# A zeroed 128x512 tile on GpSimd between the record scatters of an attention and mixture-of-experts kernel

## The chip, the cores and the metric

The kernel runs on one core of a Trainium2 chip. The metric is device microseconds (us) of one execution, the median of several runs; less is better.

## What is computed

```python
def _attn_ref(q, k, v):                       # 8 batches, 8 heads, 576 tokens, head size 64
    k_p = k.reshape(B, H, Sp, pool, D).mean(axis=3)      # pool = 8, Sp = 72
    v_p = v.reshape(B, H, Sp, pool, D).mean(axis=3)
    scores = scale * np.matmul(q, k_p.transpose(0, 1, 3, 2))
    attn = np.exp(scores - np.max(scores, axis=-1, keepdims=True))
    attn = attn / (np.sum(attn, axis=-1, keepdims=True) + 1e-09)
    return np.matmul(attn, v_p)

def _moe_ref(x, w_gate, w_noise, noise, w1, w2):  # x: 4608 tokens of 512; 8 experts of 512x1024 and 1024x512
    noisy_logits = x @ w_gate + np.log1p(np.exp(x @ w_noise)) * noise
    top2 = np.argpartition(-noisy_logits, 2, axis=1)[:, :2]
    ...
    for e in range(E):
        for k in range(2):
            mask = top2[:, k] == e
            h = np.maximum(x[mask] @ w1[e], 0.0)
            out[mask] += top2_w[mask, k, None] * (h @ w2[e])
```

The attention's output, laid out by tokens, is x of the second function. All of it is float32.

## The kernel before, in words

The program has two stages. In the first the eight batches are taken in four pairs (`pr` 0 to 3). A pair is nine chunks of 128 tokens, so there are 36 chunks. In a chunk TensorE transposes q (`qp`, L347), multiplies it by the pooled keys (`s`, L375), VectorE takes the maximum of each row (`mx`, L380), ScalarE the exponential (`ex`, L382), TensorE transposes the exponentials (`ep`, L393), ScalarE copies them out of PSUM (`eT`, L395), TensorE multiplies them by the pooled values (`a`, L408), and VectorE divides and writes the tokens (`rd` L414, `xr` L419) and their logits (`lg` L421). The string of letters in L116 sets the order in which the steps of neighbouring chunks are issued. PSUM holds two banks of each kind, so TensorE can be about a chunk ahead of the engines that empty them.

When the nine chunks of a pair are done, `route` (L494) works out for each token its two experts, its weights and its place in an expert's list. It is a generator: a few of its VectorE instructions are issued behind each following chunk, so the routing of a pair runs under the chunks of the next. For the first two pairs its opening additions (L509, L510) run on GpSimd, and VectorE's L517 waits for them. At its end it puts 18 scatters (9 columns, 2 experts for each token) into the list `scq`. A scatter (L638) is an indirect DMA that GpSimd issues: 128 records of 16 bytes go from `rec` to the rows of `rec_dram` that `pos` names. The function `advance` (L782) takes one or two from the list at fixed points of each chunk, and each scatter waits for one instruction of ScalarE or VectorE of that point:

```python
            tc.add_manual_dep(s.ins, pace[0].ins.name,
                              mybir.DependencyInfo(mybir.DependencyClass.Sync, mybir.DependencyReason.DATA),
                              reason="paced")
```

Behind the scatters of pair 1 the list holds the load of the first records (`load_recs`, L679) and the gather of the first tokens (`fetch`, `gather`, L706): GpSimd loads `raw`, then issues four indirect DMAs into `xg`. TensorE transposes these in L756, during the last two chunks of the stage. Pair 2 has the same for two more tiles. The 18 scatters of pair 3 are issued in the second stage.

In the second stage (`stage1` L1004, `stage2` L1080) each expert's tokens are multiplied by its two weight matrices. L968 sets three tiles `pv` of 128x512 to zero on GpSimd when the stage begins.

Each engine runs its own instructions in the order in which they stand in the program. GpSimd's queue in the first stage holds, apart from the scatters, the opening additions of two pairs and the gathers.

Of the kernel before, what the change touches and what calls it, by code (L numbers as in the profile page):

```python
# [8 lines left out]
F32 = mybir.dt.float32  # L9
# [10 lines left out]
def kernel(  # L20
# [12 lines left out]
    nc = tc.nc  # L33
    B, H, S, D = q.shape
    NTOK, DM = out.shape
    E = moe_w_gate.shape[1]
    DF = moe_w1.shape[2]
    P = 128
# [38 lines left out]
    rec_dram = dp.tile([E * ER, RW], I32, name="rec_dram")  # L77
# [32 lines left out]
    ap_ = ctx2.enter_context(tc.tile_pool(name="att", bufs=1))  # L110
# [379 lines left out]

    scq = []
    pace = [None]

    def route(pr, c0, c1, lg, psum):  # L494
        n = c1 - c0
# [72 lines left out]
        rec = rp.tile([P, NCH, 2, RW], I32, tag="rec", name=f"rec{pr}_{c0}", bufs=4)  # L568
# [47 lines left out]
        pos = rp.tile([P, 2, NCH], I32, tag="pos", name=f"pos{pr}_{c0}", bufs=4)  # L616
# [18 lines left out]
        V.tensor_add(word(2), later, tb)  # L635

        def scatter(c, i):
            s = nc.gpsimd.indirect_dma_start(  # L638
                out=rec_dram[:, :],
                out_offset=bass.IndirectOffsetOnAxis(ap=pos[:, i, c:c + 1], axis=0),  # L640
                in_=rec[:, c, i, :], in_offset=None)
            tc.declare_no_dep(s.ins, group="rec_scatter", reason="distinct rows")
            if pr >= NP // 2:
                tc.declare_no_dep(s.ins, group="rec_load0", reason="rows of the other half")
            if pr == NP - 1:
                tc.declare_no_dep(s.ins, group="rec_load1", reason="rows of the other pairs")
            tc.add_to_no_dep_group("rec_scatter", s.ins)
# [4 lines that stand above are left out]
        for c in range(n):  # L652
            for i in range(2):
                scq.append(lambda c=c, i=i: scatter(c, i))
# [127 lines left out]
    def advance(n, m):  # L782
        for _ in range(n):
            while gens:
                try:
                    next(gens[0])
                    break
                except StopIteration:
                    gens.pop(0)
        for _ in range(min(m, len(scq))):  # L790
            scq.pop(0)()
# [38 lines left out]
    for b in range(1, B):  # L830
        c = 9 * (b // 2) + (0 if b % 2 == 0 else 4)
# [11 lines left out]
    for b in range(2, B):  # L843
        c = 9 * ((b - 2) // 2) + (0 if b % 2 == 0 else 4)
# [87 lines left out]
            gens.append(route(pr, 0, 5, lgs[pr], one))  # L932
    due.pop()()
    advance(100, 0)
    ctx2.close()


# [308 lines left out]
    with tc.For_i(0, totr, 1) as it:  # L1246
# [5 lines left out]
        rec = op.tile([P, RW], I32, name="orec")  # L1252
# [7 lines left out]
            out=xg, out_offset=None, in_=x_dram[:, :],  # L1260
            in_offset=bass.IndirectOffsetOnAxis(ap=rec[:, 0:1], axis=0))
# [3 lines left out]
            out=pv, out_offset=None, in_=slot_dram[:, :],  # L1265
            in_offset=bass.IndirectOffsetOnAxis(ap=rec[:, 3:4], axis=0))
# [13 lines left out]
        for f in range(NFB):  # L1280
# [5 lines left out]
            out=out, out_offset=bass.IndirectOffsetOnAxis(ap=rec[:, 2:3], axis=0),  # L1286
            in_=res, in_offset=None, bounds_check=NTOK - 1, oob_is_err=False)
# [28 lines left out]
```

## Time and profile before

| what | value |
|---|---|
| median of 3 runs | 1044.02 us (1043.8 to 1044.55) |
| span of the profiled execution, first to last instruction | 1041.8 us |
| time of the profiled execution as a run | not listed apart; the median of the runs is 2.2 us above its span |
| TensorE (PE) busy | 995.3 us, 96% |
| weight loads (PEld) | 889.2 us, 85% |
| VectorE (DVE) busy | 549.0 us, 53% |
| ScalarE (ACT) busy | 345.5 us, 33% |
| GpSimd (POOL) busy | 371.0 us, 36% |
| record scatters (L638) | 72, 76.2 us, mean 1058 ns |

Busy times are sums over the whole span. The first stage ends at about 212 us, where the first matmul of L1017 stands. In a row of the timeline the first number is the start in us from the span's beginning, the second the time from the start of the first to the end of the last instruction of the row; the square bracket holds how long the engine was idle before it, and what ended that. "issue" means that the profile shows no wait that ended there, "remote" that it shows a signal but not who sent it. A matmul's end is modelled, not recorded. PEclk is the granted share of TensorE's full clock.

### The profile page before, as it was taken

The numbers are of one execution on the slowest core, as the hardware profiler recorded it, in microseconds if no ns is written. First come the engines' busy times: TensorE is split into PE (matmuls) and PEld (weight loads), VectorE is DVE, ScalarE is ACT, GpSimd is POOL, SyncE is SP. The second block draws the span as 40 slices with busy tenths as digits, with TensorE's granted clock in tenths as the row PEclk, the third lists the DMA queues.
The fourth block names the chain that finished last, engine by engine and source line by source line (L and its number), as shares of the span: only waits on it lengthen the run. The fifth ranks groups of instructions, "written<-read, shape, count | busy, mean of one in ns | idle before, by whom it ended". The sixth has DMA issues, their size and how long they took to land.

```text
span 1041.8 us, 16452 instructions
## 1 busy us (share of the span) xinstructions
PE 995.3 (96%) x5832; PEld 889.2 (85%) x5832; DVE 549.0 (53%) x1277; ACT 345.5 (33%) x857; POOL 371.0 (36%) x419
## 2 busy tenths in 40 slices
PE   7998989699999999999999999999999999999996
PEld 5897878587998898888988898889888988898995
DVE  5798768494343554554445445444554455456242
ACT  5786667541123122321232123212321232124120
POOL 4024462537310433154215421542154215421514
PEclk9999989799999999999999999999999999999999
DMA  9997853244615656577348736773577357844624
GB/s 277 336 305 235 274 155 103 82 138 118 181 60 144 211 191 191 144 242 219 111 131 249 233 120 170 249 227 100 151 248 245 116 142 258 249 137 142 203 88 136
DMA packets 137382, 190.36 MB, mean 183 GB/s; under 512 B 29155, under 2 KB 84084, under 8 KB 137274
## 3 DMA queue, kind: packets, MB, share of 16 engines
q1 hardware_dynamic: 111834, 121.84, 38.8%
q0 software_dynamic: 25440, 67.05, 20.6%
q8 instruction: 72, 1.18, 0.5%
q14 instruction: 36, 0.29, 0.1%
HBM read 126.07 MB, written 70.74 MB: 189 GB/s over the span
## 4 chain that ended last, share of the span: by engine, by line
PE 88%; issue 3%; ACT 2%; DVE 1%; DMA 1%; POOL 1%; another core or an unknown queue 1%; SPq 1%; POOLq 0%; DVEq 0%; ACTq 0%
PE bank L1017 37%; PE bank L1128 27%; PE bank L1094 10%; PE a L408 5%; PE s L375 3%; PE ep L393 2%; PE qp L347 2%; ACT ex L382 1%; DMA v<-in_v_dram 1%; ACT eT L395 1%; POOL out_dram L1073 1%; PE kT L298 0%; PE vr L325 0%; SPq L219 0%
## 5 line engine op out<-in xcount | busy, mean ns | idle before, releaser
L1017 PE MATMUL bank<-xh,w 128*128 128x512 f32 (+6 forms) x1536 | 390.4, 338 | 0.6 <-issue 0.6
L1017 PEld LDWEIGHTS bank<-xh,w 128*128 128x128 f32 x1536 | 270.3, 188 | 21.4 <-issue 0.9
L1128 PE MATMUL bank<-w,hh 128*128 128x512 f32 x880 | 271.7, 390 | 1.3 <-issue 1.2
L1017 PE MATMUL bank<-xl,w 128*128 128x512 f32 (+6 forms) x768 | 259.7, 338 | 1.2 <-issue 0.9
L1028 ACT ACTIVATE hh<-bank 128x512 fp32r<-128x512 f32 (+4 forms) x192 | 96.7, 510 | 459.9 <-PE bank L1017 369.2
L1029 DVE SCALAR_TENSOR_TENSOR hl<-bank,hh 128x512 fp32r<-128x512 f32 (+4 forms) x192 | 110.1, 579 | 243.1 <-ACT hh L1028 212.7
L1128 PEld LDWEIGHTS bank<-w,hh 128*128 128x128 f32 x880 | 164.8, 188 | 34.8 <-issue 1.1
L1128 PE MATMUL bank<-w,hl 128*128 128x512 f32 x440 | 171.4, 390 | 1.0 <-issue 1.0
L1017 PEld LDWEIGHTS bank<-xl,w 128*128 128x128 f32 x768 | 144.6, 188 | 11.3 <-DVE xl L767 0.6
L1065 DVE SCALAR_TENSOR_TENSOR pv<-bank,raw,pv 128x128 f32<-128x128 f32 x196 | 55.5, 342 | 111.8 <-DMA pv<-slot_dram,raw 51.8
L1069 POOL DMA_DIRECT2D slot_dram<-yt x17 | 9.8, 576 | 276.0 <-DVE yt L1065 225.5
L638 POOL DMA_INDIRECT rec_dram<-rec,pos x72 | 76.2, 1058 | 85.3 <-DVE rec L635 26.9
L1094 PE MATMUL bank<-hh,w 128*128 128x240 f32 (+3 forms) x512 | 103.6, 298 | 2.2 <-issue 1.7
L1128 PEld LDWEIGHTS bank<-w,hl 128*128 128x128 f32 x440 | 82.6, 188 | 19.5 <-issue 2.4
L1049 POOL DMA_INDIRECT pv<-slot_dram,raw x70 | 68.7, 982 | 62.4 <-DMA slot_dram<-ys 34.2
L481 DVE TENSOR_TENSOR w<-wst,w 128x512 fp32r<-128x512 f32 x128 | 82.6, 682 | 11.1 <-ACT w L480 10.6
L1094 PEld LDWEIGHTS bank<-hh,w 128*128 128x128 f32 x512 | 82.6, 189 | 2.7 <-issue 2.1
L480 ACT CAST w<-wst 128x512 fp32r<-128x512 f32 x128 | 73.0, 618 | 27.1 <-DMA wst<-in_moe_w_dram 27.1
L715 POOL DMA_INDIRECT row<-x_dram,raw x70 | 70.2, 1004 | 21.3 <-issue 20.7
L1069 POOL DMA_DIRECT2D slot_dram<-pv x55 | 31.7, 576 | 125.1 <-DVE pv L1065 89.2
L1094 PE MATMUL bank<-hl,w 128*128 128x320 f32 (+3 forms) x256 | 76.0, 297 | 0.0
L382 ACT ACTIVATE ex<-s,mx 128x72 f32<-128x72 f32 x288 | 70.8, 342 | 12.8 <-DVE mx L380 7.5
(165 smaller groups left out, 1032.3 us busy)
## 6 DMA issues: line engine op xcount, KB each, us to landing
wst<-in_moe_w_dram SPq DMA_DIRECT2D x64, 512.0 KB
via<-row SPq DMA_DIRECT2D x266, 64.0 KB
xg<-via SPq DMA_DIRECT2D x63, 256.0 KB
slot_dram<-pv POOLq DMA_DIRECT2D x55, 256.0 KB
k<-in_k_dram SPq DMA_DIRECT2D x7, 1280.0 KB
v<-in_v_dram SPq DMA_DIRECT2D x16, 512.0 KB
x_dram<-xr SPq DMA_DIRECT2D x16, 512.0 KB
q<-in_q_dram SPq DMA_DIRECT2D x7, 1024.0 KB
```

The costliest lines, as they stand in the source:

```text
L382: lasta[0] = nc.scalar.activation(ex[:, jj, EPOS[h] * G:(EPOS[h] + 1) * G], sv[:, i], AF.Exp, bias=mx[:, i:i + 1])
L480: nc.scalar.copy(hv, sv)
L481: nc.vector.tensor_sub(lv, sv, hv.bitcast(F32))
L638: s = nc.gpsimd.indirect_dma_start(out=rec_dram[:, :], out_offset=bass.IndirectOffsetOnAxis(ap=pos[:, i, c:c + 1], axis=0), in_=rec[:, c, ...
L715: turn_of("pool", lambda: nc.gpsimd.indirect_dma_start(out=row[:32 * nr], out_offset=None, in_=x_dram[:, :], in_offset=bass.IndirectOffset ...
L1017: nc.tensor.matmul(part(ph), w1s(e, a, db, f), part(xs[b][:, db]), start=(i == 0), stop=(i == 3 * NDB - 1))
L1028: act = nc.scalar.activation(hh[:, :n], ph[:, :n], AF.Relu)
L1029: last = nc.vector.scalar_tensor_tensor(hl[:, :n], ph[:, :n], 0.0, hh[:, :n].bitcast(F32), op0=OP.max, op1=OP.subtract)
L1049: turn_of("pool", lambda: nc.gpsimd.indirect_dma_start(out=pv[:np_], out_offset=None, in_=slot_dram[:P + e * CAP, :], in_offset=bass.Indir ...
L1065: nc.vector.scalar_tensor_tensor(r_, y_, wc, pv[:plain] if plain else r_, op0=OP.mult, op1=OP.add)
L1094: nc.tensor.matmul(part(py), w2s(e, b, f)[:, mb * P:(mb + 1) * P], part(hs[f][a]), start=(i == 0), stop=(i == 3 * NFB - 1))
L1128: mm = nc.tensor.matmul(py, hs[f][a][:, cs], w2s(e, b, f), start=(i == 0), stop=(i == 3 * NFB - 1))
```

## The change

Between two scatters that are taken from the list during the first stage, GpSimd sets a new tile, `spacer` (128x512 float32), to zero. The zeroing is ordered directly behind the scatter before it, and the next scatter behind the zeroing. Nothing reads the tile. From the end of the first stage on (`attending[0] = False`) the scatters are issued as before.

```diff
     scq = []
     pace = [None]
+    tail_rec = [None]
+    attending = [True]
+    spacer = ap_.tile([P, DM], F32, name="spacer")
...
         def scatter(c, i):
-            s = nc.gpsimd.indirect_dma_start(
-                out=rec_dram[:, :],
-                out_offset=bass.IndirectOffsetOnAxis(ap=pos[:, i, c:c + 1], axis=0),
-                in_=rec[:, c, i, :], in_offset=None)
+            def put():
+                return nc.gpsimd.indirect_dma_start(
+                    out=rec_dram[:, :],
+                    out_offset=bass.IndirectOffsetOnAxis(ap=pos[:, i, c:c + 1], axis=0),
+                    in_=rec[:, c, i, :], in_offset=None)
+
+            if attending[0] and tail_rec[0] is not None:
+                with tc.issue_after(tail_rec[0].ins), tc.issue_after(pace[0].ins):
+                    gap = nc.gpsimd.memset(spacer, 0.0)
+                with tc.issue_after(gap.ins):
+                    s = put()
+            else:
+                s = put()
+            tail_rec[0] = s
             tc.declare_no_dep(s.ins, group="rec_scatter", reason="distinct rows")
...
     due.pop()()
     advance(100, 0)
+    attending[0] = False
     ctx2.close()
```

On GpSimd this is what stands in the order at the end of pair 0's scatters, where the opening additions of pair 1 follow. `rec_dram<-rec_0` is a scatter, `lg_834` are the logits of pair 1. Before:

```order
L510 TENSOR_TENSOR rt_0_1_830<-lg_286 128x16
L638 DMA rec_dram<-rec_0_986,pos_0_1131 37376x4 x11
L509 TENSOR_TENSOR lg_834<-lg_834 128x8x64
L509 TENSOR_TENSOR lg_834<-lg_834 128x8x32
L510 TENSOR_TENSOR rt_0_1_1473<-lg_834 128x128
```

With the change, from the last but one of these eleven scatters on:

```order
L642 DMA rec_dram<-rec_0_987,pos_0_1132 37376x4
L649 MEMSET spacer 128x512
L642 DMA rec_dram<-rec_0_987,pos_0_1132 37376x4
L649 MEMSET spacer 128x512
L512 TENSOR_TENSOR lg_835<-lg_835 128x8x64
L512 TENSOR_TENSOR lg_835<-lg_835 128x8x32
L513 TENSOR_TENSOR rt_0_1_1484<-lg_835 128x128
```

Eleven zeroings now stand among and behind the eleven scatters, ahead of the additions; the zeroing that belongs to the twelfth scatter stands ahead of the additions, not beside its scatter.

The second place is the end of the first stage, where GpSimd turns from pair 2's scatters to the tiles of the second stage (`pv`) and to the second load of records (`raw_4`). Before:

```order
L638 DMA rec_dram<-rec_0_2292,pos_0_2435 37376x4 x16
L968 MEMSET pv_2760 128x512
L968 MEMSET pv_2762 128x512
L968 MEMSET pv_2764 128x512
L638 DMA rec_dram<-rec_0_2292,pos_0_2435 37376x4 x2
L679 DMA raw_4_2789<-rec_dram 128x8
```

With the change:

```order
L649 MEMSET spacer 128x512
L642 DMA rec_dram<-rec_0_2328,pos_0_2471 37376x4
L982 MEMSET pv_2812 128x512
L982 MEMSET pv_2814 128x512
L982 MEMSET pv_2816 128x512
L642 DMA rec_dram<-rec_0_2328,pos_0_2471 37376x4 x2
L692 DMA raw_4_2841<-rec_dram 128x8
```

Sixteen of pair 2's scatters have a zeroing ahead of them, the last two have none. In all there are 51 zeroings; the instructions of the other four engines stand in the same order as before.

## Rows read from the trace of the kernel before

**Rows 1.** The page: span, busy time, and TensorE's granted clock in 40 slices.

```profile
span 1041.8 us, 16452 instructions
PE 995.3 (96%) x5832; PEld 889.2 (85%) x5832; DVE 549.0 (53%) x1277; ACT 345.5 (33%) x857; POOL 371.0 (36%) x419
PEclk9999989799999999999999999999999999999999
```

**Rows 2.** Stretches: length, busy PE, PEld, DVE, ACT, POOL; clock, DMA share, GB/s.

```profile
20.00:88.00 68.00, 65.63 (x563) 57.79 (x564) 56.48 (x154) 51.83 (x179) 5.45 (x6) 1.00 0.98 322
88.00:213.00 125.00, 102.81 (x786) 91.63 (x787) 85.30 (x266) 79.51 (x264) 64.16 (x63) 0.89 0.52 155
```

**Rows 3.** Instruction groups, 88 to 213 us: the scatters.

```profile
L638 POOL DMA_INDIRECT rec_dram<-rec,pos x52 | 55.7, 1071 | 71.3 <-DVE rec L635 23.5 <-DVE rd L415 18.6 <-issue 11.6
```

**Rows 4.** Timeline of GpSimd: the first and last scatter of a burst, and the next.

```profile
186.52 1.00 POOL L638 DMA_INDIRECT rec_dram<-rec,pos  x1 [15.79 <-DVE rec L635]
...
200.62 0.96 POOL L638 DMA_INDIRECT rec_dram<-rec,pos  x1 [0.30 <-issue]
205.17 1.36 POOL L638 DMA_INDIRECT rec_dram<-rec,pos  x1 [3.59 <-DVE lg L421]
```

**Rows 5.** Timeline of the other engines, 194 to 206 us.

```profile
195.21 0.63 PE L393 MATMUL ep<-ident,ex 128*112 128x128 f32 x2
203.66 1.98 PE L756 MATMUL xp<-ident,xg 128*128 128x128 f32 x8 [7.83 <-ACT eT L395]
203.03 0.59 ACT L395 COPY eT<-ep 112x512 f32<-112x512 f32 x1 [7.80 <-remote]
205.69 0.59 ACT L767 CAST xh<-xp 128x512 fp32r<-128x512 f32 x1 [0.27 <-PE xp L756]
203.77 0.17 DVE L414 TENSOR_SCALAR rd<-a 128x8 f32<-128x8 f32 x1 [8.74 <-remote]
```

**Rows 6.** Timeline, 97 to 147 us: an earlier burst's end, and TensorE in another.

```profile
97.42 0.66 PE L347 MATMUL qp<-ident,q 128*128 128x128 f32 x4
99.93 0.97 POOL L638 DMA_INDIRECT rec_dram<-rec,pos  x1 [0.30 <-ACT ex L382]
101.13 0.59 ACT L349 COPY qT<-qp 128x512 f32<-128x512 f32 x1 [1.50 <-PE s L375]
101.77 1.28 PE L393 MATMUL ep<-ident,ex 128*112 128x128 f32 x6 [1.33 <-issue]
146.93 0.47 PE L347 MATMUL qp<-ident,q 128*128 128x128 f32 x1 [2.06 <-issue]
```

**Rows 7.** Stretches at the lower clock, columns as in rows 2.

```profile
102.56:105.97 3.41, 3.41 (x15) 3.41 (x16) 2.01 (x7) 2.78 (x11) 1.91 (x2) 0.50 0.95 288
146.93:157.17 10.24, 8.63 (x36) 8.04 (x37) 4.43 (x9) 4.72 (x16) 7.75 (x7) 0.50 0.33 121
194.72:208.37 13.65, 5.82 (x25) 5.41 (x26) 4.05 (x9) 4.19 (x10) 7.67 (x8) 0.50 0.22 62
```

**Rows 8.** Timeline of GpSimd: zeroings of 128x512.

```profile
6.62 0.51 POOL L167 MEMSET zt<- 128x512 f32 x1
213.10 1.47 POOL L968 MEMSET pv<- 128x512 f32 x3
```

**Rows 9.** Timeline, 103 to 114 us: GpSimd before pair 1's additions, and who waits.

```profile
103.45 0.97 POOL L638 DMA_INDIRECT rec_dram<-rec,pos  x1 [2.55 <-DVE lg L421]
109.15 2.67 POOL L509 TENSOR_TENSOR lg<-lg 128x512 f32<-128x512 f32 x2 [3.15 <-DVE lg L421]
113.98 0.23 DVE L517 SCALAR_TENSOR_TENSOR rt<-rt 128x72 f32<-128x72 f32 x1 [0.47 <-POOL rt L510]
```

**Rows 10.** Timeline of GpSimd: first load of records, last gather, last scatters of pair 2.

```profile
163.49 0.59 POOL L679 DMA_DIRECT2D raw<-rec_dram  x1 [1.42 <-DMA rec_dram<-rec,pos]
169.78 0.95 POOL L706 DMA_INDIRECT xg<-x_dram,raw  x1 [0.30 <-issue]
219.65 0.97 POOL L638 DMA_INDIRECT rec_dram<-rec,pos  x1 [5.07 <-DVE rt L555]
```

## Prediction

> **What bounds the kernel now.** I read the page first. TensorE is busy for 96% of the span, but the granted clock is below its highest digit in two slices of the first fifth (8 and 7) and in the last one [rows 1]. So I cut the first stage into stretches. From 20 to 88 us TensorE is busy for 65.63 of 68.00 us; from 88 to 213 us for 102.81 of 125.00, at a mean clock of 0.89 [rows 2]. The second stretch is the one in which the scatters run: 52 of them, 55.7 us of GpSimd [rows 3]. From 20 to 88 us GpSimd works for 5.45 us in all [rows 2].
>
> Then I looked at the holes themselves. At 195.84 us (195.21 + 0.63) TensorE has finished the transposes `ep`; ScalarE, which has nothing else to do, copies them at 203.03, and VectorE takes up the product `a` at 203.77. TensorE waits for that copy for 7.83 us [rows 5]. All through this time GpSimd issues scatters: twelve of them from 186.52 to 200.62 us, one every 1.28 us (14.10 / 11), with 0.30 us between two [rows 4]. The three engines go on within 2.2 us of the end of the last one (201.58). A few us later, after GpSimd has paused for 3.59 us and issues a single scatter at 205.17 [rows 4], ScalarE starts 0.05 us behind TensorE (203.66 + 1.98 = 205.64, then 205.69) [rows 5]. The same pattern stands in an earlier burst: `qp` is done at 98.08 us, its copy starts at 101.13 though ScalarE is free for 1.50 us before, and TensorE stands idle for 1.33 us before 101.77; the burst's last scatter ran from 99.93 to 100.90. In the burst of pair 1 there is an idle time of 2.06 us before 146.93 [rows 6]. So what I read is: while scatters follow each other closely, the others learn late that TensorE is done, and TensorE then runs out of free PSUM banks.
>
> The idle times have a second price. The clock falls from 2.4 to 1.2 GHz (0.50) in three stretches of 3.41, 10.24 and 13.65 us, each beginning at or just behind such a hole [rows 7].
>
> **What there is to gain.** Idle time from 88 to 213 us: 125.00 - 102.81 = 22.2 us. At the idle share of 20 to 88 us (2.37 / 68 = 3.5%) it would be 4.4 us, so 17.8 us are in excess. TensorE is busy for 3.41 + 8.63 + 5.82 = 17.9 us at half clock [rows 7]; at full clock at most half of that goes, 8.9 us. Together 26.7 us, if every delay went.
>
> **The change, part by part.**
>
> A zeroing costs GpSimd 0.49 us in a row of three (1.47 / 3), 0.51 us alone [rows 8]. The trace has none between two scatters; if the 0.30 us that stands before a scatter came twice, it would be 0.81 us. So the 51 zeroings add 25 to 41 us to GpSimd, which idles for 125.00 - 64.16 = 60.8 us in this stretch [rows 2]: it has room, and its own time costs nothing by itself. I take 0.49, since the three zeroings in a row follow the scatter before them without a gap.
>
> What the zeroing does to a burst: it lengthens the step from 1.28 to 1.77 us, so that scatters fill 55% of a burst (0.97 / 1.77) in place of 76%, and 0.80 us are free of them in place of 0.31. About 38 of the 52 scatters have nothing but the queue before them (11.6 us of "issue" at 0.30 us each [rows 3]); there it separates. Where the next scatter waits for its pace or for the records anyway, the zeroing runs inside that wait and separates nothing.
>
> How much of the 26.7 us that gives back is the open term. Its ends are nothing (a free time of 0.31 us did not let the signals through in the last burst [rows 4, 5]) and all of it (after a pause of 3.59 us they came in 0.05 us). For a middle speak two things. By the share that scatters fill, the way from 76% to 55% is nearly half of the way to 21% (0.97 of 0.97 + 3.59). And the delay does not come at once: the burst that begins at 186.52 us costs its first long hole only in its second half, and the arrears are gone 2.2 us after its end. If they are arrears that pile up, they grow by about 0.2 us for each of eleven scatters, less than the 0.49 us that a zeroing gives. I take 60%, between "half" and "all": 16.0 us.
>
> In this part a rule of the Trainium skill speaks against the change. Its page "SBUF — State Buffer", section "Who interferes with whom", says that only VectorE and GpSimd share a port pair and that TensorE and ScalarE never wait on anyone. By it scatters could not hold up TensorE's signals, the sum would be 0, and the time 1044. The rows on the burst at 186 us [rows 4, 5] speak for a link that it does not have; no run so far shows the cause.
>
> What comes later on GpSimd. In pair 0 eleven zeroings (5.4 us) now stand ahead of pair 1's opening additions. GpSimd had 2.55 + 3.15 = 5.7 us of waits there, so at today's times the additions are not late; VectorE waits 0.47 us for them [rows 9]. If 60% of the first burst's loss goes (1.33 us idle, 1.7 us of clock: 1.8 us), what they need comes 1.8 us earlier and they start about 1.5 us after that; VectorE stands in its queue at L517, with the maxima and divisions of the next chunk behind it. I charge 1.0 us. In pair 1 eighteen zeroings move the load of records from 163.49 to about 172 us and the end of the last gather from 170.7 to 179.6 us [rows 10]; TensorE wants those tiles at 195.84 us, or about 10 us earlier if the bursts are relieved: hidden. In pair 2 sixteen zeroings (7.8 us) run against a wait of 5.07 us ahead of the last two scatters [rows 10] and earlier waits such as 3.59 us [rows 4]: hidden. The tile itself takes 2 KB of each partition for nothing that waits.
>
> **Sum.** 1044.0 - 16.0 + 1.0 = **1029.0 us**. The working is against the profiled execution, whose span is 1041.8 us; the runs' median lies 2.2 us above it, and I carry that over unchanged.
>
> **Rivals.**
>
> *All delays go.* If the holes are arrears, a step of 1.77 us lets none build up. 1044.0 - 26.7 = 1017.3. For it: the quick end of the holes behind each burst. Against it: ScalarE and VectorE would have to keep TensorE's pace as from 20 to 88 us, and pair 1's additions become a wait.
>
> *Nothing changes.* The holes come from something else that happens at these times, or a zeroing keeps the path as busy as a scatter does; GpSimd's time is hidden. 1044. For it: the rule above, and that late signals are also absent beside some scatters. Against it: three bursts, three holes, three falls of the clock.
>
> *Slower: longer bursts.* The delays last as long as GpSimd works off its list, whatever is between two scatters. The loss then grows with the length of a burst, by 1.77 / 1.28 = 1.38: 26.7 x 0.38 = 10.1 us, 1054.2. It decides where the loss for each us of a burst stays above 1 / 1.38 = 72% of today's. For it: 0.31 us between two scatters let nothing through for five scatters on end [rows 4, 5], and 0.80 us is nearer to 0.31 than to 3.59. Against it: zeroing needs no DMA, and GpSimd's 5.45 us of plain work before 88 us [rows 2] stand in a stretch without such holes.
>
> **How the numbers follow.** Part of the delays goes, 1029: 0.40, with a range of its own of 1022 to 1039 (a share of 80% to 20%, rounded). All go, 1017: 0.20. Nothing, 1044: 0.17. Slower, up to 1054: 0.23. A measurement of this kernel tells apart about 0.2%, 2 us. Faster: 0.40 + 0.20 = 0.60; same 0.17; slower 0.23. Cases of both signs hold much of the chance, so the range is wide: 1016 to 1054, which leaves out a twentieth below and about a tenth above.
>
> **What would show it.** In the new profile the scatters of a burst should start 1.7 to 1.8 us apart; 1.3 would mean that the zeroing is hidden, 2.1 the upper price. In the stretch from 88 us to the first matmul of L1017 the idle time of TensorE should fall from 22 to some 11 to 12 us, and the three stretches at half clock should become one or none. ScalarE's wait for `ep` with a "remote" end, 7.80 us now, should be gone or below 2 us. VectorE's wait for L510 should rise by 1 to 2 us. I am wrong in the mechanism if the step is 1.77 us and the idle time stays, and wrong in sign if holes as long as today's stand in longer bursts. If the time falls and the first stage is as long as before, the gain came from elsewhere and the working does not hold.

## Result: faster in the first comparison, slower on another chip

The change took 1031.31 us (median of 9 runs, 1027.72 to 1036.81), the kernel before 1043.8 us beside it (9 runs, 1037.65 to 1046.55): ratio 0.9892, 95% interval 0.9863 to 0.9921. The gain is small, 1.1%, but no run of the one overlaps with one of the other. The forecast was 1029.0. The profiled execution of the change took 1028.72 us, one of its quicker ones, with a span of 1026.9 us against 1041.8: the traces show a gain of 14.9 us, the medians one of 12.5.

That is half of the result. The later runs came from chips that their results number (that of the first comparison is not on record), and the kernel before has two times there: 1007.64 us (chip 9) and 1006.9 us (chip 11), but 1044.45 and 1041.69 us (chip 4) and 1045.02 us (chip 0). Where it takes 1007 us the change is **slower**: 1017.72 us on chip 11, ratio 1.0106 (1.008 to 1.0131). Ratios are of the faster runs alone: on chip 4 five of the 13 runs behind 1044.45 us are over 1.5% above the fastest and are left out of the ratio, not of the median. The reason given for the gain, TensorE's signals arriving late beside close scatters, is in the traces of one kind of chip and absent from the other.

The page of the change (span, busy time), against [rows 1]:

```profile
span 1026.9 us, 16502 instructions
PE 995.0 (97%) x5832; PEld 891.8 (87%) x5832; DVE 549.2 (53%) x1277; ACT 344.8 (34%) x857; POOL 402.7 (39%) x470
```

TensorE's busy time is the same to 0.3 us; what went is idle time. GpSimd works 31.7 us more. From 88 us to the first matmul of the second stage, the kernel before and then the change (columns as in [rows 2]):

```profile
88.00:212.03 124.03, 102.18 (x785) 91.31 (x785) 84.33 (x264) 79.51 (x264) 63.30 (x62) 0.89 0.52 155
...
88.00:194.82 106.82, 97.67 (x787) 88.76 (x785) 84.83 (x267) 79.12 (x265) 85.15 (x100) 0.94 0.61 181
```

TensorE's idle time there is 9.15 us, where it was 21.85. More stretches of the change, the bursts of pairs 1 and 2 and the three at half clock:

```profile
136.60:171.00 34.40, 33.37 (x294) 30.89 (x292) 31.11 (x94) 28.34 (x97) 31.55 (x36) 1.00 0.49 146
179.80:211.00 31.20, 28.45 (x163) 24.44 (x162) 24.46 (x79) 17.37 (x47) 28.20 (x36) 0.95 0.45 125
114.03:124.27 10.24, 9.16 (x52) 8.65 (x53) 7.71 (x27) 5.46 (x19) 6.58 (x8) 0.50 0.77 264
185.71:189.13 3.42, 3.42 (x17) 3.10 (x16) 2.49 (x8) 2.62 (x8) 3.09 (x5) 0.50 0.12 37
243.74:253.98 10.24, 7.82 (x31) 6.71 (x31) 1.20 (x4) 0.82 (x3) 5.04 (x7) 0.50 0.38 66
```

The first row is the whole of pair 1's burst, 18 scatters with their zeroings: TensorE idles for 1.03 of 34.40 us at full clock. In the kernel before, pair 1's burst ran without a longer pause for 15 of its 18 scatters, and behind its hole the clock fell [rows 6, 7]:

```profile
135.20:156.50 21.30, 16.93 (x99) 15.02 (x98) 11.81 (x23) 12.75 (x43) 17.02 (x15) 0.78 0.55 162
```

So pair 1's spaced burst is clean. Pair 2's is less so: TensorE idles for 2.75 of 31.20 us. The three stretches at half clock of the change stand in other places, and its timeline shows what stands beside them:

```profile
110.65 2.07 POOL L512 TENSOR_TENSOR lg<-lg 128x512 f32<-128x512 f32 x2
...
114.18 0.23 DVE L520 SCALAR_TENSOR_TENSOR rt<-rt 128x72 f32<-128x72 f32 x1 [4.51 <-POOL rt L513]
115.11 0.46 PE L393 MATMUL ep<-ident,ex 128*112 128x128 f32 x1 [2.99 <-ACT ex L382]
...
143.62 0.98 POOL L642 DMA_INDIRECT rec_dram<-rec,pos  x1 [0.17 <-issue]
144.59 0.54 POOL L649 MEMSET spacer<- 128x512 f32 x1
145.30 2.35 POOL L642 DMA_INDIRECT rec_dram<-rec,pos  x1 [0.16 <-issue]
...
182.65 1.04 ACT L395 COPY eT<-ep 112x512 f32<-112x512 f32 x2 [2.18 <-PE a L408]
...
194.82 0.47 PE L1031 MATMUL bank<-xh,w 128*128 128x512 f32 x1
...
242.96 1.13 DVE L1081 TENSOR_SCALAR pv<-bank,raw 128x128 f32<-128x128 f32 x4 [11.64 <-remote]
```

The step of a burst is 1.68 us (145.30 - 143.62): a scatter of 0.98, the zeroing of 0.54, and 0.17 before the next. At 110.65 us the opening additions of pair 1 follow pair 0's last zeroing (110.15 + 0.54) with no wait of their own, so they are late; VectorE stands at L520 for 4.51 us (0.47 before [rows 9]), TensorE for 2.99 us behind it, and half clock follows. From 174.6 to 184 us the four gathers, which have no zeroing between them, and the first scatters of pair 2 follow each other without a pause; there TensorE has holes of 1.03, 1.31 and 0.78 us, ScalarE takes up a copy late (at 182.65 us), and 3.42 us at half clock follow. At 242 us, beside pair 3's scatters, which have no zeroing either, VectorE's long wait again has a "remote" end, TensorE has holes of 1.12 and 1.03 us, and the third stretch at half clock follows.

The second stage begins at 194.82 us, 17.2 us sooner; the span is 14.9 us shorter, so 2.3 us were given back in the second stage.

### The profile page after: what moved, and what is told of

Its sections match the earlier page's. It is cut to its first block, busy times and chain, and to the rows that moved or that the text cites. A ratio compares the mean times of both kernels' runs of the same rounds, so it can differ in the third digit from the quotient of the medians.

```text
span 1026.9 us, 16502 instructions
## 1 busy us (share of the span) xinstructions
PE 995.0 (97%) x5832; PEld 891.8 (87%) x5832; DVE 549.2 (53%) x1277; ACT 344.8 (34%) x857; POOL 402.7 (39%) x470
## 4 chain that ended last, share of the span: by engine, by line
PE 89%; POOL 3%; issue 3%; ACT 2%; DVE 1%; DMA 1%; SPq 0%; POOLq 0%; ACTq 0%; DVEq 0%
PE bank L1031 38%; PE bank L1142 28%; PE bank L1108 10%; PE a L408 4%; PE s L375 3%; PE ep L393 2%; PE qp L347 2%; POOL rec_dram L642 1%; ACT ex L382 1%; ACT eT L395 1%; POOL out_dram L1087 1%; ACT kbd L302 0%; DVE k L233 0%; PE vr L325 0%; PE kT L298 0%
## 5 line engine op out<-in xcount | busy, mean ns | idle before, releaser
L642 POOL DMA_INDIRECT rec_dram<-rec,pos x72 | 80.9, 1124 | 42.4 <-DVE rd L415 18.6
L1142 PEld LDWEIGHTS bank<-w,hl 128*128 128x128 f32 x440 | 82.6, 188 | 17.2
L728 POOL DMA_INDIRECT row<-x_dram,raw x70 | 72.2, 1031 | 21.3 <-issue 20.1
```

What stands on the lines that cost most here:

```text
L642: return nc.gpsimd.indirect_dma_start(out=rec_dram[:, :], out_offset=bass.IndirectOffsetOnAxis(ap=pos[:, i, c:c + 1], axis=0), in_=rec[:, ...
L728: turn_of("pool", lambda: nc.gpsimd.indirect_dma_start(out=row[:32 * nr], out_offset=None, in_=x_dram[:, :], in_offset=bass.IndirectOffset ...
L1142: mm = nc.tensor.matmul(py, hs[f][a][:, cs], w2s(e, b, f), start=(i == 0), stop=(i == 3 * NFB - 1))
```

## Experiments

Diffs are against the change unless they say otherwise. Line numbers of the change are 3 to 14 higher than those before.

### What the scatters cost at all (four kernels, chip 9)

No scatters in pairs 0 to 2 (against the kernel before; the records of these pairs are not written):

```diff
         def scatter(c, i):
+            if pr < NP - 1:
+                return
```

> The kernel before without the 52 record scatters of pairs 0 to 2 (they are left out, so the experts of those tokens get no records; all other instructions stay). Theory (close scatters hold up TensorE's signals): the holes of TensorE and the stretches at half clock between 88 us and the second stage go, TensorE's idle time there falls from 22 us to about 5 us, the second stage begins at about 185 to 190 us instead of 212, and the run takes 1016 to 1024 us. Rival (the holes come from something else that happens at that time): the holes stay, second stage at about 210 us, 1040 us or more.

GpSimd busy without DMA (against the kernel before; a copy of one column of places and two zeroings of 128x512 instead of each scatter, which is left out):

```diff
+            if pr < NP - 1:
+                s = nc.gpsimd.tensor_copy(busy[:, :1], pos[:, i, c:c + 1])
...
+                    nc.gpsimd.memset(busy, 0)
+                    nc.gpsimd.memset(busy, 0)
+                return
```

> The kernel before with each of the 52 scatters of the first stage replaced by a copy of one column and two zeroings of 128x512 on GpSimd, with the same waits (records of pairs 0 to 2 are not written). GpSimd is about as busy as before, at a step of 1.2 to 1.3 us, but issues no indirect DMA. Theory: like the run without scatters, second stage at 185 to 192 us, 1016 to 1026 us. Rival (a busy GpSimd, or its waits on the paced instructions, holds up the others, whatever it does): holes as in the kernel before, second stage near 205 to 212 us, 1036 to 1044 us.

A zeroing of one column:

```diff
-                    gap = nc.gpsimd.memset(spacer, 0.0)
+                    gap = nc.gpsimd.memset(spacer[:, :1], 0.0)
```

> The change with a zeroing of 128x1 in place of 128x512 between the scatters: the same instructions in the same order and the same tile, hardly any time. Theory (the free time between two scatters decides): step about 1.3 to 1.4 us, most of the holes of the kernel before come back, second stage at 204 to 212 us, 1036 to 1044 us. Rival (any instruction between two scatters breaks the chain, or the tile's place in memory matters): like the change, second stage at about 195 us, 1028 to 1034 us.

Two zeroings between scatters:

```diff
                     gap = nc.gpsimd.memset(spacer, 0.0)
+                with tc.issue_after(gap.ins):
+                    gap = nc.gpsimd.memset(spacer, 0.0)
```

> The change with two zeroings of 128x512 between two scatters: step about 2.2 us. Theory: no holes from scatters at all, but pair 1's opening additions on GpSimd come about 5 us later than in the change and VectorE waits 5 us or more for them, and the last gather ends near 190 us; second stage at 193 to 203 us, 1028 to 1038 us. Rival (a step of 1.7 us is not yet enough and more room gives more): second stage at 186 to 190 us, 1020 to 1025 us.

Measured: 1006.4, 1004.86, 1006.9 and 1047.65 us, and **the kernel before 1007.64 us** (25 runs, 1004.3 to 1012.38). The expectations were worked out for a kernel before of 1044 us. Against the one that ran beside them the first three say that on this chip there was next to nothing to win: ratios 0.9983 (0.996 to 1.0007), 0.9972 (0.9948 to 0.9996) and 0.999 (0.997 to 1.0011). Taking all 52 scatters away is worth no more than 0.4%. So these runs cannot tell the theory from its rivals: the late signals that they were to take away were not there. Neither kernel without scatters ran on a chip that has them.

The fourth was expected at 1028 to 1038 us and is 4.1% slower than the kernel before (1.0354 to 1.0471). Its timeline:

```profile
120.84 0.23 DVE L520 SCALAR_TENSOR_TENSOR rt<-rt 128x72 f32<-128x72 f32 x1 [12.16 <-POOL rt L513]
121.77 0.46 PE L393 MATMUL ep<-ident,ex 128*112 128x128 f32 x1 [10.63 <-ACT ex L382]
...
195.54 1.02 POOL L721 DMA_INDIRECT xg<-x_dram,raw  x1 [4.10 <-DMA raw<-rec_dram]
199.11 1.10 PE L771 MATMUL xp<-ident,xg 128*128 128x128 f32 x4 [10.20 <-DMA xg<-x_dram,raw]
...
251.32 1.13 PE L771 MATMUL bank<-ident,xg 128*128 128x128 f32 x4 [9.04 <-DMA xg<-x_dram,raw]
```

Three holes of 9.0 to 10.6 us, none of which ends with a late signal: the first waits for the additions that stand behind pair 0's list, the other two for gathers that stand behind the lists of pairs 1 and 2. VectorE's wait, foreseen as 5 us or more, was 12.16. This is the price that lies in GpSimd's queue: with one zeroing a part of it is paid (next section), and the second adds 51 x 0.54 = 27.5 us to the queue and makes the kernel about 30 us slower than the first (on chips 9 and 11).

### The two kernels and the pair 0 term on one chip (chip 11)

The kernel before and the change, unchanged:

> The kernel before, unchanged, to have its trace on the chip of this comparison. Theory A (GpSimd's close scatters hold up TensorE's signals in every execution, the chip does not matter): about 1044 us, ScalarE and VectorE learn 1 to 8 us late of TensorE's ends at 144 to 157 and 192 to 204 us, three stretches at half clock. Theory B (the late signals belong to the chip or to the program's placement in memory, not to the scatters alone; the comparison with 1007.64 us for the kernel before speaks for it): about 1007 us, no late signal over 0.8 us beside the same scatters 1.28 us apart, TensorE idle under 4 us of 88 to 213 us.

> The change, unchanged, beside the kernel before on one chip. Theory A: 0.989 of the kernel before, as in the first comparison. Theory B: the zeroings have a cost of their own that does not depend on the late signals: additions of pair 1 and gathers late on GpSimd (gaps of TensorE of 2.99, 1.04, 1.31, 0.78 and 3.00 us, and 10.24 + 3.41 + 10.24 us at half clock in the trace of the change, worth 9.1 + 11.9 = 21 us). Where the kernel before has no late signals this makes the change about 2% slower: 1025 to 1031 us against 1007.

The zeroing of one column once more, and the change without pair 0's zeroings (`if attending[0] and pr > 0 and tail_rec[0] is not None`):

> The change with a zeroing of one column, 128x1 words (0.12 us instead of 0.54), a scatter every 1.28 us as in the kernel before. If the kernel before is at 1044 us on this chip: theory A (it is the free time that counts, and there is none here) gives 1044 us again; a rival (any other instruction between two scatters is enough) gives about 1007 us. If the kernel before is at 1007 us here, both give 1004 to 1010 us, as the same kernel gave 1006.9 in the comparison ahead of this one.

> The change without the zeroings of pair 0 (those of pairs 1 and 2 stay). The additions of pair 1 then start at about 105 us instead of 110.65 us. Theory B: the 2.99 us gap of TensorE at 112 us and the 10.24 us at half clock behind it go, 8 us less than the change. Theory A: the same 8 us less, and on a chip with late signals 1 to 3 us back for pair 0's own scatters (half clock of 3.41 us at 102.56 us in the kernel before). A rival (the half clock at 114 us has another cause than the late additions): no change against the change, within 2 us.

Measured: 1005.97, **1017.72**, 1006.44 and 1012.5 us beside 1006.9. Theory A, that every execution has late signals, falls. Theory B holds in its sign; its price for the change, 1025 to 1031 us, was 7 to 13 us too high. Whether it is the chip or the program's placement in memory, which theory B named side by side, these runs do not separate. The kernel before, its stretches (all of the scatters' time, then pair 1's burst) and timeline:

```profile
88.00:213.00 125.00, 122.06 (x929) 108.33 (x929) 110.86 (x358) 93.11 (x294) 80.65 (x78) 1.00 0.63 192
129.50:156.20 26.70, 26.64 (x234) 25.02 (x234) 24.16 (x61) 24.47 (x86) 21.52 (x18) 1.00 0.51 150
```

```profile
142.03 0.97 POOL L638 DMA_INDIRECT rec_dram<-rec,pos  x1 [0.30 <-issue]
143.31 0.97 POOL L638 DMA_INDIRECT rec_dram<-rec,pos  x1 [0.30 <-DVE vbd L327]
...
182.03 0.48 PE L1017 MATMUL bank<-xh,w 128*128 128x512 f32 x1
```

The scatters are the same, 0.97 us every 1.28 us with 0.30 between them, and there are more of them without a pause. Beside them TensorE idles for 0.06 of 26.70 us, and from 80 to 265 us neither ScalarE nor VectorE has a wait of 0.4 us or more with a "remote" end. The second stage begins at 182.03 us, 30 us ahead of the same kernel in the first comparison. The change on the same chip:

```profile
91.73 1.52 POOL L642 DMA_INDIRECT rec_dram<-rec,pos  x1 [18.63 <-DVE rd L415]
...
118.00 0.33 PE L393 MATMUL ep<-ident,ex 128*112 128x128 f32 x1 [2.98 <-ACT ex L382]
...
224.54 0.75 PE L769 MATMUL bank<-ident,xg 128*128 128x128 f32 x4 [1.07 <-DMA xg<-x_dram,raw]
226.74 0.75 PE L769 MATMUL bank<-ident,xg 128*128 128x128 f32 x4 [1.45 <-DMA xg<-x_dram,raw]
```

```profile
29.63:36.45 6.82, 6.62 (x44) 5.71 (x45) 2.49 (x3) 4.03 (x14) 0.00 (x0) 0.50 1.07 345
118.37:121.79 3.42, 3.42 (x29) 3.15 (x27) 2.15 (x8) 1.61 (x7) 1.80 (x3) 0.50 1.03 385
227.60:231.01 3.41, 3.41 (x10) 2.65 (x9) 0.69 (x1) 0.51 (x1) 2.75 (x3) 0.50 0.06 7
```

The span is 9.5 us longer (1015.2 against 1005.7), and it comes apart into three. The first scatter starts at 91.73 us in place of 89.00: 2.7 us are lost before any zeroing has run, behind the stretch at half clock from 29.63 us. The kernel before has no such stretch in its trace, but the kernel without scatters on chip 9, which has no zeroings, has one too (30.9 to 37.7 us at 0.52), so this part is not the zeroings'; whether every execution has it is not known. From the first scatter to the second stage, which begins at 189.55 us, another 4.8 us are lost; the hole of 2.98 us and half of 3.42 us make 4.7. The remaining 2.0 us are lost in the second stage, where TensorE waits for gathers that stand behind pair 2's list; the two holes and half of 3.41 us come to 4.2 us there, but the kernel before has idle time of its own (1.82 us from 300 to 500 us, where the change has none). Where the signals are prompt, the change has its costs alone, about 6.8 of the 9.5 us in these traces.

Without pair 0's zeroings 5.2 us of the loss go (1017.72 to 1012.5). Expected were 8, by the half clock of 10.24 us in the first trace; here it lasts 3.42 us. VectorE waits for the additions as little as in the kernel before:

```profile
113.54 0.23 DVE L520 SCALAR_TENSOR_TENSOR rt<-rt 128x72 f32<-128x72 f32 x1 [0.47 <-POOL rt L513]
...
185.22 0.48 PE L1031 MATMUL bank<-xh,w 128*128 128x512 f32 x1
```

The rival, that the half clock has another cause, falls: hole and half clock at 118 us went together. Here too the first scatter is late (92.24 us) without a zeroing ahead of it, and the second stage begins as much later than in the kernel before (185.22 against 182.03 us): in this trace the zeroings of pairs 1 and 2 cost the first stage nothing.

### Free time, or any instruction between two scatters? (chip 4)

```diff
-                    gap = nc.gpsimd.memset(spacer, 0.0)
+                    gap = nc.gpsimd.memset(spacer if pr == 2 else spacer[:, :1], 0.0)
```

> The change with the zeroing cut to one column (128x1) between the scatters of pairs 0 and 1; those of pair 2 keep 128x512. Where the kernel before runs at about 1007 us: theory C (pair 0's zeroings cost 5.2 us through the additions of pair 1, pair 1's the other 5.6 us through the record load and the gathers behind the scatters, pair 2's nothing, since no engine waits for its last scatter before the second stage is far on) gives 1005 to 1009 us, first L1031 matmul at 182 to 183 us; the rival (pair 2's zeroings are what is left) gives 1010 to 1013 us. Where the kernel before runs at about 1044 us: if free time is what counts, the half clock at 147 to 157 us is back and the time is over 1030 us; if any instruction between two scatters is enough, no late signal over 0.8 us at 88 to 160 us and 1008 to 1020 us.

Measured: 1046.48 us beside 1044.45 (ratio 1.0047, 1.0008 to 1.0086), so this chip has the late signals. One execution has both kinds of burst: pair 1's with one column (12 of its scatters, up to the first longer pause), then pair 2's with 128x512, all of it.

```profile
137.40:154.90 17.50, 11.38 (x77) 9.96 (x75) 10.04 (x20) 9.57 (x33) 15.36 (x24) 0.87 0.57 167
193.20:223.60 30.40, 29.48 (x181) 25.55 (x180) 27.08 (x84) 18.51 (x50) 27.43 (x36) 1.00 0.46 120
```

```profile
149.93 0.11 POOL L649 MEMSET spacer<- 128x1 f32 x1
149.97 0.58 ACT L395 COPY eT<-ep 112x512 f32<-112x512 f32 x1 [3.78 <-remote]
150.60 1.12 PE L347 MATMUL qp<-ident,q 128*128 128x128 f32 x4 [3.46 <-issue]
...
202.72 0.86 ACT L395 COPY eT<-ep 112x512 f32<-112x512 f32 x2 [0.16 <-PE ep L393]
```

With a tiny zeroing TensorE idles for 35% of the burst and ScalarE waits 3.78 us with a "remote" end; with the full one TensorE idles for 3%, and the same copy starts 0.16 us after ScalarE's last work. Behind the burst with one column half clock is back, 10.24 us of it from 150.6 us. Pair 2's burst, spaced in the same way, lost 2.75 of 31.20 us in the first comparison, where the gathers ran straight into it; here they end at 177.2 us, 16 us ahead of it, and it loses 0.92 of 30.40. An instruction between two scatters is not enough; the time free of scatters does it, or the lower rate of scatters that comes with it, which no run separates. The part of theory C on a chip without late signals stayed untried, since this was none; but its "pair 2's nothing" does not fit the traces of chip 11, where the holes of the second stage wait for gathers behind pair 2's list.

### Half the zeroing; and other pairs (chip 4)

Half of it (`memset(spacer[:, :DM // 2], 0.0)`):

> The change with half the zeroing (128x256 words, about 0.3 us) in pairs 0 to 2. Step in a burst about 1.45 us, 0.48 us free of scatters, between the 0.30 of the kernel before and the 0.71 of the change. Where the kernel before has late signals (about 1044 us): if what is missing is free time in proportion, between 1031 and 1046 us (about 1038), with late signals of 1 to 3 us left in pair 1's burst; if there is a point above which the signals keep up and 0.48 us lies over it, about 1028 us, none over 0.8 us. Where the kernel before has none (about 1007 us): half of the change's 10.8 us of loss or less, 1008 to 1014 us.

None in pair 0, and two of 128x192 in pair 3:

```diff
-            if attending[0] and tail_rec[0] is not None:
+            if pr and spacer[0] is not None and tail_rec[0] is not None:
...
-                    gap = nc.gpsimd.memset(spacer, 0.0)
+                    gap = nc.gpsimd.memset(spacer[0], 0.0)
+                    if pr == NP - 1:
+                        gap = nc.gpsimd.memset(spacer[0], 0.0)
...
+    spacer[0] = mp.tile([P, 192], F32, name="spacer2")
```

> The change without the zeroings of pair 0, and with zeroings added between the scatters of pair 3 too (two of 128x192 words each, since there is no room for 128x512 in that stage). Where the kernel before has late signals: the first stage loses 1 to 3 us to pair 0's scatters and wins 8 us since pair 1's additions are no longer late; the second stage wins the 3.0 us of gaps and 5.1 us of half clock beside pair 3's scatters: 1015 to 1024 us, about 0.98 of the kernel before. A rival (the gaps beside pair 3 come from something else): no gain in the second stage, 1024 to 1030 us. Where the kernel before has no late signals: about 1012 us as without pair 0's zeroings, or up to 5 us more if pair 3's scatters delay what stands behind them in GpSimd's queue.

Measured: 1026.53 us (0.9846, 0.9795 to 0.9896) and 1027.74 us (0.9858, 0.9817 to 0.9899) beside 1041.69. Half the zeroing, stretches of the bursts of pairs 1, 2 and 3, and timeline:

```profile
136.70:165.60 28.90, 27.22 (x236) 25.25 (x235) 22.84 (x54) 23.90 (x85) 26.09 (x36) 1.00 0.47 139
184.60:212.20 27.60, 23.70 (x139) 21.24 (x139) 19.89 (x60) 14.99 (x43) 24.60 (x36) 0.94 0.35 107
223.00:247.80 24.80, 24.59 (x112) 20.09 (x110) 11.74 (x40) 5.19 (x10) 19.57 (x20) 1.00 0.46 126
```

```profile
189.11 0.98 POOL L642 DMA_INDIRECT rec_dram<-rec,pos  x1 [0.16 <-issue]
190.09 0.33 POOL L649 MEMSET spacer<- 128x256 f32 x1
190.58 0.98 POOL L642 DMA_INDIRECT rec_dram<-rec,pos  x1 [0.17 <-issue]
...
192.70 1.25 PE L769 MATMUL xp<-ident,xg 128*128 128x128 f32 x8 [1.84 <-issue]
192.74 0.17 DVE L414 TENSOR_SCALAR rd<-a 128x8 f32<-128x8 f32 x1 [2.30 <-remote]
...
202.72 0.48 PE L1031 MATMUL bank<-xh,w 128*128 128x512 f32 x1
...
238.95 0.59 ACT L780 CAST xh<-bank 128x512 fp32r<-128x512 f32 x1 [7.44 <-remote]
```

The step is 1.47 us with 0.49 free, and the late signals are smaller, not gone: in pair 2's burst a hole of 1.84 us where the kernel before had 7.83 [rows 5], and 5.8% idle in pair 1's, where the largest hole is 0.88 us. That is the answer "in proportion" by the idle shares; of the delays of 1 to 3 us that it foresaw in pair 1's burst there are none. The time is that of the other answer all the same (1028), for another reason: the second stage begins at 202.72 us, 7.9 us later than with the change in the first comparison, but pair 3's burst, which neither kernel spaces, costs nothing in this execution (24.59 of 24.80 us busy), though ScalarE there has a wait of 7.44 us with a "remote" end. So a close burst does not always cost time on such a chip. That late signals cost time only where TensorE runs out of other work fits this, and was not tried apart.

The other kernel, pair 1's burst with the full zeroing on this chip, and its second stage:

```profile
137.60:172.00 34.40, 33.42 (x294) 30.90 (x292) 31.14 (x94) 28.30 (x97) 31.54 (x36) 1.00 0.49 144
```

```profile
263.17 1.13 PE L771 MATMUL bank<-ident,xg 128*128 128x128 f32 x4 [3.90 <-DMA xg<-x_dram,raw]
```

The holes beside pair 3's scatters are gone (TensorE is busy for all of the 35.30 us from 221.30), and one of 3.90 us stands in their place, with 6.82 us at half clock behind it: TensorE waits for a gather that stands behind the longer burst. The forecast of 1015 to 1024 us was too low. It priced the late signals and not what stands behind the burst; and in this trace the first stage lost more than it had foreseen, 6.83 us at half clock from 184.06 us, where the gathers run into pair 2's first scatters, and a first scatter at 92.44 us in place of 88.83, ahead of all zeroings.

### Half, in pairs 1 and 2 alone (chip 0)

> Half the zeroing (128x256 words), and only between the scatters of pairs 1 and 2. Where the kernel before has late signals (about 1042 us): against the half zeroing in pairs 0 to 2 (1026.5 us) the 2.06 us gap at pair 1's additions and 5.1 us of the half clock behind it go, and pair 0's own late signals cost 2 to 4 us again (gaps of 0.56, 0.62, 0.68 and 1.20 us in the trace without pair 0's zeroings): 1021 to 1027 us, ratio 0.98 to 0.985. A rival (what pair 0's burst loses is as much as the late additions cost): 1027 to 1032 us. Where the kernel before has none (about 1007 us): less than the 5.6 us that 128x512 in pairs 1 and 2 cost there, 1006 to 1010 us.

Measured: 1030.64 us beside 1045.02, ratio 0.9898 (0.9847 to 0.995). The hole at pair 1's additions is gone and the first stage has no half clock from 88 us on, but pair 0's burst and, in the second stage, pair 3's lose again:

```profile
87.70:101.00 13.30, 11.34 (x86) 9.90 (x86) 10.09 (x19) 9.72 (x34) 10.85 (x9) 1.00 0.64 149
133.00:163.10 30.10, 28.39 (x243) 26.02 (x241) 24.70 (x63) 24.59 (x86) 27.29 (x36) 1.00 0.43 133
212.10:239.50 27.40, 23.27 (x101) 18.15 (x100) 13.08 (x44) 5.84 (x11) 21.57 (x22) 0.94 0.50 143
```

The time is the rival's, 1027 to 1032; its reason is not shown, since pair 3's burst, spaced in neither kernel, lost 4.13 us here and 0.21 us in the execution with half the zeroing in three pairs. The intervals of this kernel, of the change, of half the zeroing and of the one with pair 3 in place of pair 0 overlap, so no version was shown to beat the change where signals are late. Where they are prompt, none that does the whole computation was faster than the kernel before.

## Why the prediction was right, and where it was not

**The mechanism** (close scatters let the others learn late that TensorE is done) holds on the chip of the first comparison and on chips 4 and 0, and not on 9 and 11. That it is the closeness of the scatters rests on the graded spacing, since no kernel without scatters ran where signals are late. Pair 1's burst, by the time free of scatters in a step (for 0.30 us with late signals up to the first longer pause, 15 and 12 of the 18 scatters):

| kernel, chip | free of scatters | TensorE idle in the burst | clock |
|---|---|---|---|
| before, first comparison | 0.30 us | 4.37 of 21.30 us, 21% | 0.78 |
| one column, chip 4 | 0.30 us | 6.12 of 17.50 us, 35% | 0.87 |
| 128x256, chip 4 | 0.49 us | 1.68 of 28.90 us, 5.8% | 1.00 |
| 128x256, chip 0 | 0.49 us | 1.71 of 30.10 us, 5.7% | 1.00 |
| 128x512, first comparison | 0.71 us | 1.03 of 34.40 us, 3.0% | 1.00 |
| 128x512, chip 4 | 0.71 us | 0.98 of 34.40 us, 2.8% | 1.00 |
| before, chip 11 | 0.30 us | 0.06 of 26.70 us, 0.2% | 1.00 |

**The step** of 1.77 us was 1.68: 0.54 for the zeroing in place of 0.49, but 0.17 and not 0.30 before the scatter.

**The share of 60%** was too low for the spaced bursts: in pair 1's nearly all delays went, as the rival "all delays go" had it. ScalarE's wait with a "remote" end is gone from the first stage; VectorE has one of 2.41 us left, beside pair 2's first scatters. One of the two grounds for the share was misread: the way from 76% to 55% is 38% of the way to 21%, not nearly half (and a share of 80% gives 1023.6 us, not 1022). The idle time from 88 us to the second stage fell from 21.9 to 9.15 us, somewhat further than foreseen (11 to 12), but 6.1 us of what is left belong to places that the prediction had priced at little or nothing.

**The late additions** were the mis-sized term: 1.0 us was charged, and 2.99 us of hole and half of 9.16 us at half clock make 7.6. The step that failed is "they start about 1.5 us after that". The additions ended only 0.2 us later than in the kernel before (114.15 against 113.94 us, the ends of L513 and L510), but with pair 0's burst relieved VectorE came to them 3.84 us earlier, not 1.8, and waited for 4.51 us; and the charge left out that TensorE then stands behind VectorE, and that the clock falls when it does. "Hidden" for the gathers held in the first stage in so far as TensorE waits for no gather there; what it did not foresee is that the gathers, issued later, run straight into pair 2's scatters: there stand the holes of 1.03, 1.31 and 0.78 us and the stretch of 3.42 us at half clock.

**Half clock** did not go: 20.4 us of TensorE's work (9.16 + 3.42 + 7.82) were done at it, 17.9 before [rows 7]. "One or none" was wrong: two such stretches stand ahead of the second stage and one in it. So that 1029.0 came out so close is luck in part: two errors met, a share too low and a cost too low. The sign and the range rest on the mechanism, and on this kind of chip.

**The rival "nothing changes"** drew on the Trainium skill's page "SBUF — State Buffer", section "Who interferes with whom", by which TensorE and ScalarE never wait on anyone. The traces of chip 11 agree with what the rival made of it (0.06 us idle in a burst of 26.70); those of the first comparison and of chips 4 and 0 do not. That section speaks of ports, and no run here shows at what the signals are held up, so what failed is the step from ports to signals. Nor was GpSimd's time hidden, as the rival had it: on chip 11 the change cost 1.06%. The rival "longer bursts" had the right sign for chip 11, and for two zeroings on chip 9, with the wrong mechanism: what grows with the burst is not the delay of signals but the lateness of what is queued behind it.

**Open:** why chips differ, and whether it is the chips. Within a comparison all runs of the kernel before are of one kind, the scatters have the same duration and step on both kinds, and chip 4 was of the same kind in two comparisons; but something else that stays the same through a comparison, such as where the program lies in memory, was not ruled out. The change as it is ran beside late signals in the first comparison alone, its variants on chips 4 and 0. What holds the signals up beside the scatters was not found either; no kernel here separates the issue of an indirect DMA from its packets.

## What to carry to other kernels

An engine that has idle time still has a queue: before filling it, look at what stands behind the filling and who waits for that; here one zeroing between scatters made the kernel 10.8 us slower where nothing was won (about 6.8 us by that queue, as far as the traces show), and two made it 40 us slower. Where a profile shows a wait with a "remote" end beside a burst of indirect DMAs, look at the same kernel on another chip before building a cure: the sign of this change depended on it. Free time between the scatters cures it; how much, and in which bursts, trades against that queue, and the versions run here could not be told apart.

## What the runs showed of the hardware

- The kernel before takes 1003.6 to 1012.4 us on two chips (58 runs) and 1030.7 to 1054.9 us on others; no run lies between (one of 4228.66 us on chip 4 is left out of all this). Of the difference of 36 us between the spans of the two traces (1041.8 and 1005.7), 30 lie in the first stage.
- On the second kind what TensorE loses beside indirect DMAs depends on the time free between them, from burst to burst of one execution: on chip 4 it idled for 35% of a burst with 0.30 us free and for 3% of one with 0.71 us.
- A zeroing of 128x1 words took 0.11 us on GpSimd, of 128x256 0.33 and of 128x512 0.54, and the scatter behind one started 0.16 to 0.19 us later, against 0.30 behind another scatter.
- A hole of TensorE of 2.98 us was followed by 3.42 us at half clock on one chip, and one of 2.99 us by 10.24 us on another.
